# Attention and feed-forward on one core: prologue dealt out anew, late q moved, six weight chunks loaded as fp32 and cast on VectorE and GpSimd

## The chip, the cores and the metric

The kernel runs on one core of a Trainium2 chip. The metric is the time of one execution on the device in microseconds (us). A core has TensorE (PE; its weight loads are shown apart as PEld), VectorE (DVE), ScalarE (ACT), GpSimd (POOL), SyncE (SP, which here only issues transfers) and 16 DMA engines. Two queues carry the data in the traces: the hardware queue, filled by SyncE, and the software queue, filled by GpSimd (31.87 and 4.98 MB in the kernel before). Each profile is of one execution; its span is some 1.7 us shorter than the device time of the same execution. Kernels are compared only within the same rounds.

## The reference, cut to what matters

```python
# q, k, v: (B=4, H=8, S=768, D=64) fp32; w_in: (512, 2048); w_out: (2048, 512)
k_sum = k.reshape(B, H, nb, 32, D).max(axis=3)      # nb = 24 blocks
v_sum = v.reshape(B, H, nb, 32, D).mean(axis=3)
# each query sees the keys at a distance under 16, and all 24 block summaries (+ log 32)
a = softmax([where(mask_l, scores_l, -1e9), scores_s + log(32)])
attn_out = a @ concat(v, v_sum)
x = attn_out.transpose(0, 2, 1, 3).reshape(3072, 512)
h = x @ w_in
g = h * (1 / (1 + exp(-1.702 * h)))
out = g @ w_out                                     # (3072, 512) fp32
```

## The kernel before

The work is cut into eight units, each half a sequence of one batch. The attention of the first half has no other work to hide behind; this "prologue" ends near 23 us. Then each unit runs the first product ("ph", 64 matmuls of 128x384) and the second ("po", 48 matmuls of 128x512 in 12 slots of four), and the attention of the next half sits between these slots. In unit 0 the slots go by parts: all three row blocks use the first w_out chunk, then all three the second, and so on, because the chunks arrive one after another.

Weights come through the software queue. The load itself changes fp32 to bf16 on its way (such a load writes 512.0 KB a chunk in the kernel before):

```python
def load_w_in(c):                    # 4 chunks of 512 columns
    pool.dma_start(out=w_in_sb[:, :, c*512:(c+1)*512], in_=wi[:, :, c*512:(c+1)*512])
def load_w_out(c):                   # 4 chunks of 512 rows
    pool.dma_start(out=w_out_sb[:, c*4:(c+1)*4, :], in_=wo[:, c*4:(c+1)*4, :])
# ... after the hand-dealt prologue:
load_w_in(2)
for p in range(NP): load_q(0, p, 1)  # "late q": second half of batch 0's queries, fp32
load_w_in(3)
for c in range(4): load_w_out(c)
```

The late q is cast by VectorE, turned by TensorE against an identity, and copied out of PSUM by VectorE, all within unit 0's first product (after its columns 11 to 14). GpSimd issues every load of weights between its other instructions, in program order; in the traces here GpSimd and VectorE also work through their instructions in program order. `idle(n)` puts n small matmuls without use into TensorE's waits in the prologue; `busy(n)` does it with a PSUM tile of its own.

The loads of batch 1 stand behind a small copy whose only purpose is to wait for a late w_out chunk, so that they don't compete with the weights:

```python
if u == 0 and i == 1:
    sp.dma_start(out=hold, in_=w_out_sb[0:16, NT - 5, 0:16])   # third w_out chunk
    for p in range(NP): load_k(1, p)
    load_v(1)
```

The softmax here doesn't subtract the row's maximum and nothing guards it: scores larger than these inputs give would overflow.

## Time and profile before

| of the kernel before | value |
|---|---|
| median of runs (lowest to highest) | 221.47 us (221.15 to 221.71), 3 runs |
| profiled span, granted TensorE clock | 219.3 us, 1.000 |
| TensorE busy | 206.6 us, 94% |
| first "ph" matmul; first "po" matmul | 23.29 us; 37.19 us |
| hold copy; unit 1's first "ph" | 42.15 us; 50.67 us |
| waits of TensorE over 0.3 us in unit 0 | 0.40 + 0.79 + 0.35 us |

The table is read from the top down: TensorE is nearly always busy, so time can be won or lost only where it waits or where its instructions take longer. After 80 us neither happens. What a change to the start does to the end can therefore be read off at one instant, unit 1's first matmul at 50.67 us. The lines themselves stand in the prediction below.

### The profile page before, as it was taken

Reading aid. Unit: us, or ns where it says so; the run is one execution under the profiler, and the core shown is the slowest. Engines: PE = TensorE matmul, PEld = TensorE weight load, DVE = VectorE, ACT = ScalarE, POOL = GpSimd, SP = SyncE. Lnnn points to the kernel's source line nnn. Section 1 sums busy time; section 2 is a strip of 40 time slices with the busy share of each in tenths; the row PEclk is TensorE's granted clock in tenths of the full one; section 3 lists DMA queues with packets and bytes.
Section 4 is the critical chain, followed back from the end, with each engine's and each line's share of the span. In section 5 each row is a group of like instructions: output and inputs, shape, how many; then the busy total and the mean of one; then the engine's idle time right before and its main releaser. Section 6 shows DMA issues by size and latency. Waiting matters only on the chain.

```text
span 219.3 us, 4951 instructions
## 1 busy us (share of the span) xinstructions
PE 206.6 (94%) x1944; PEld 115.7 (53%) x1966; DVE 93.9 (43%) x261; ACT 136.9 (62%) x243; POOL 69.1 (32%) x169
## 2 busy tenths in 40 slices
PE   7679998999999999999999999999999999999994
PEld 3247554556655556454655465545554554555542
DVE  5997645345994830176707100549226001700000
ACT  3786775456577647862888277835786478637420
POOL 5579985014784029400600079004100000000000
PEclk9999999999999999999999999999999999999999
DMA  6999999999998999799699999998904300340012
GB/s 165 313 216 145 191 262 223 184 199 220 233 323 210 225 231 256 136 231 210 128 209 226 218 224 217 211 192 199 193 3 104 115 0 0 87 122 13 0 48 96
DMA packets 92710, 37.15 MB, mean 169 GB/s; under 512 B 77856, under 2 KB 89568, under 8 KB 92688
## 3 DMA queue, kind: packets, MB, share of 16 engines
q1 hardware_dynamic: 88272, 31.87, 71.2%
q0 software_dynamic: 4416, 4.98, 12.9%
q8 instruction: 15, 0.25, 0.5%
q14 instruction: 7, 0.06, 0.1%
HBM read 27.26 MB, written 6.29 MB: 153 GB/s over the span
## 4 chain that ended last, share of the span: by engine, by line
PE 81%; DMA 9%; SPq 3%; POOL 3%; issue 2%; DVE 1%; DVEq 0%; POOLq 0%
PE po L27 37%; PE ph L27 33%; DMA w_out_sb<-in_moe_w_out_dram 7%; PE ps_av L27 4%; SPq L27 3%; PE ps_s L27 3%; DMA vf<-in_v_dram 2%; PE ps_q L27 1%; POOL kx L27 1%; POOL vw L27 1%; PE ps_t L27 1%; DVE qT L27 1%; POOL w_in_sb L27 1%; PE ps_vs L27 1%; PE ps_x L27 1%
## 5 line engine op out<-in xcount | busy, mean ns | idle before, releaser
L27 PE MATMUL po<-w_out_sb,gT 128*128 128x512 bf16 (+2 forms) x378 | 86.3, 370 | 2.6 <-issue 1.6
L27 PE MATMUL ph<-xT,w_in_sb 128*128 128x384 bf16 x512 | 86.5, 326 | 0.8 <-DMA w_in_sb<-in_moe_w_in_dram 0.8
L27 ACT ACTIVATE gT<-ph 128x384 bf16<-128x384 f32 x128 | 60.9, 491 | 26.1 <-PE ph L27 26.0
L27 PEld LDWEIGHTS <-w_in_sb 128*128 128x128 bf16 x512 | 49.4, 98 | 33.3 <-DMA w_in_sb<-in_moe_w_in_dram 1.0
L27 PEld LDWEIGHTS <-gT 128*128 128x128 bf16 x400 | 36.3, 98 | 38.9 <-DMA w_out_sb<-in_moe_w_out_dram 0.7
L27 DVE TENSOR_TENSOR a_sb<-a_sb,mk 128x768 bf16<-128x768 bf16 x32 | 17.6, 555 | 66.5 <-ACT a_sb L27 65.4
L27 ACT ACTIVATE osb<-po 128x512 f32<-128x512 f32 (+1 forms) x24 | 14.2, 592 | 37.0 <-PE po L27 36.8
L27 ACT ACTIVATE a_sb<-ps_s 128x768 bf16<-128x768 f32 x32 | 24.2, 805 | 7.2 <-PE ps_s L27 7.2
L27 POOL CAST vw<-vf 128x768 bf16<-128x768 f32 (+3 forms) x36 | 24.8, 742 | 3.5 <-DMA vf<-in_v_dram 3.1
L27 ACT ACT_TABLE_LOAD x16 | 20.5, 1283 | 1.1 <-PEq L1029 0.8
L27 POOL COPY gate<-gT 128x1 bf16<-128x1 bf16 x4 | 0.8, 190 | 60.5 <-ACT gT L27 60.5
L27 POOL CAST kb<-kf 128x768 bf16<-128x768 f32 (+1 forms) x15 | 11.1, 766 | 17.6 <-DMA kf<-in_k_dram 17.6
L27 DVE TENSOR_TENSOR x<-ps_av,rc 128x384 bf16<-128x384 f32 x28 | 15.6, 558 | 1.0
L27 PEld LDWEIGHTS <-a_sb 128*64 128x64 bf16 x384 | 7.9, 111 | 6.9 <-issue 4.0
L27 DVE TENSOR_REDUCE ks<-kx 128x24 bf16<-128x768 bf16 x12 | 11.3, 939 | 0.1
L27 DVE COPY osb<-po 128x128 f32<-128x128 f32 x1 | 0.3, 292 | 24.9 <-PE po L27 24.9
L27 DVE COPY kx<-kx 128x80 bf16<-128x80 bf16 (+4 forms) x48 | 10.6, 272 | 0.0
L27 PE MATMUL ps_av<-vw,a_sb 128*64 128x65 bf16 x384 | 9.9, 198 | 0.5 <-DVE x_sb L27 0.5
L27 PE MATMUL ps_s<-qT,kx 64*128 64x64 bf16 x384 | 9.3, 191 | 1.0 <-POOL kx L27 0.6
L27 PEld LDWEIGHTS <-kx 64*128 64x128 bf16 x384 | 7.0, 95 | 5.4 <-issue 3.9
L27 DVE RECIPROCAL rc<-ps_av 128x6 f32<-128x6 f32 x32 | 6.1, 190 | 8.1 <-PE ps_av L27 8.1
L27 POOL CAST qb<-qf 128x768 bf16<-128x768 f32 (+1 forms) x13 | 8.9, 716 | 0.9 <-PE ps_q L27 0.8
(71 smaller groups left out, 126.1 us busy)
## 6 DMA issues: line engine op xcount, KB each, us to landing
out_dram<-osb SPq DMA_DIRECT2D x23, 256.0 KB, 3.1
kf<-in_k_dram SPq DMA_DIRECT2D x12, 384.0 KB, 5.7
vf<-in_v_dram SPq DMA_DIRECT2D x12, 384.0 KB, 5.7
qf<-in_q_dram SPq DMA_DIRECT2D x8, 384.0 KB, 5.7
w_in_sb<-in_moe_w_in_dram POOLq DMA_DIRECT2D x4, 512.0 KB, 7.6
w_out_sb<-in_moe_w_out_dram POOLq DMA_DIRECT2D x4, 512.0 KB, 17.1
kf<-in_k_dram SPq DMA_DIRECT2D x8, 192.0 KB, 4.0
qf<-in_q_dram SPq DMA_DIRECT2D x8, 192.0 KB, 3.8
```

Of the source, the lines that this page charges most:

```text
L27: r = f(*a, **kw)
```

## The change

It has three parts, called P, Q and W here.

- **P**: the prologue's casts, copies and turns are dealt out anew between the engines, and the values and x get PSUM tiles of their own. GpSimd reaches its first weight load sooner.
- **Q**: the late q is loaded behind the first w_out chunk, and its four turns move from the first product into slots 1 and 2 of the second. Their copies out of PSUM go to VectorE (turns 0 and 2) and ScalarE (1 and 3).
- **W**: two w_in chunks and all four w_out chunks are loaded as they are, in fp32, into the memory that held k, q and v of batch 0, and cast there by VectorE (both w_in chunks, w_out 0 and 1) and GpSimd (w_out 2 and 3). The apparent intent is to take the conversion out of the software queue and the weights off its critical path.

```diff
+    raws = stage.tile([128, 3 * NP * PR], F32, name="raws")      # k, q, v of all loads
+    room = {("i", 2): 0, ("i", 3): 2048, ("o", 0): 4096, ("o", 1): 6144, ("o", 2): 0, ("o", 3): 4096}
+    def cast_w_in(eng, c):      # 4 casts of 4 x 128 columns
+    def cast_w_out(eng, c, n=2):
     def load_w_out(c):
-        pool.dma_start(out=w_out_sb[:, c * 4:(c + 1) * 4, :],
+        pool.dma_start(out=roomy("o", c),
  ... (prologue: P, some 130 lines re-ordered)
-    load_w_in(2)
+    load_w_in(2, True)
+    load_w_in(3, True)
+    load_w_out(0)
     for p in range(NP):
         load_q(0, p, 1)
-    load_w_in(3)
-    for c in range(4):
-        load_w_out(c)
  ... (v casts on GpSimd)
+    load_w_out(1)
     vrows0()                    # block rows of v, and the halo and sum copies within SBUF
+    cast_w_in(dve, 2)
+    load_w_out(2)
  ... (key halos, pairs 0 and 1)
+    cast_w_in(dve, 3)
  ... (key halos, pairs 2 and 3)
+    cast_w_out(dve, 0)
+    load_w_out(3)
+    for p in range(NP):
+        cast_q(dve, p, 1)
+    cast_w_out(dve, 1)
     finish_masks()              # GpSimd
  ... (clears on GpSimd)
+    cast_w_out(pool, 2)
+    cast_w_out(pool, 3, 1)
-    plan0 = {0: ["s0", "s1"], 4: ["v0", "s2"], 6: ["x0", "s3"], 9: ["v1"], 11: ["x1"]}
+    plan0 = {1: ["q0", "q1"], 2: ["q2", "q3"], 3: ["s0", "s1"], 5: ["v0", "s2"], 7: ["x0", "s3"],
+             9: ["v1"], 11: ["x1"]}
+            elif what[0] == "q":
+                q_turn(i, 1)
+                q_copy(i, act if i % 2 else dve, 1)
-                sp.dma_start(out=hold, in_=w_out_sb[0:16, NT - 5, 0:16])
+                sp.dma_start(out=hold, in_=w_out_sb[0:16, NT - 7, 0:16])
```

More of the change, by code (lines that the diff above doesn't have):

```diff
@@ L81 @@
     raw, late = {}, [None]
+    PR = 2 * NJ * D
+    raws = stage.tile([128, 3 * NP * PR], F32, name="raws")
     def chunks(x, b, p):
@@ L87, in load_k @@
     def load_k(b, p):
-        t = stage.tile([128, 2, 2, JH, D], F32, name=f"kf{p}", tag=f"kf{p}")
+        t = (raws[:, p * PR:(p + 1) * PR]
+             .rearrange("p (h e r d) -> p h e r d", h=2, e=2, r=JH))
         if b:
@@ L99, in load_q @@
         if half is None:
-            t = stage.tile([128, 2, NJ, D], F32, name=f"qf{p}", tag=f"qf{p}0")
+            t = (raws[:, (NP + p) * PR:(NP + p + 1) * PR]
+                 .rearrange("p (h j d) -> p h j d", h=2, j=NJ))
             sp.dma_start(out=t.rearrange("p h j d -> p (h j) d"), in_=chunks(q, b, p))
@@ L109, in load_q @@
         t = (late[0][:, p] if half else
-             stage.tile([128, 2, JH, D], F32, name=f"qf{p}0", tag=f"qf{p}0"))
+             raws[:, (NP + p) * PR:(NP + p) * PR + PR // 2]
+             .rearrange("p (h r d) -> p h r d", h=2, r=JH))
         raw["q", p, half] = t
@@ L119, in load_v @@
         for p in range(NP):
-            t = stage.tile([128, 2, NJ, D], F32, name=f"vf{p}", tag=f"vf{p}")
+            t = (raws[:, (2 * NP + p) * PR:(2 * NP + p + 1) * PR]
+                 .rearrange("p (h j d) -> p h j d", h=2, j=NJ))
             if b:
@@ L237, in clear0, with roomy, load_w_in @@
             eng.memset(v6[g * 32:g * 32 + nb, :, g, D:D + 1], float(block))
-    def load_w_in(c):
+    room = {("i", 2): 0, ("i", 3): 2048, ("o", 0): 4096, ("o", 1): 6144, ("o", 2): 0, ("o", 3): 4096}
+    def roomy(kind, c):
+        o = room[kind, c]
+        return raws[:, o:o + 2048].rearrange("p (a n) -> p a n", a=4)
+    def cast_w_in(eng, c):
+        for i in range(4):
+            o = c * 512 + i * 128
+            copy(eng, w_in_sb[:, :, o:o + 128], roomy("i", c)[:, :, i * 128:(i + 1) * 128])
+    def cast_w_out(eng, c, n=2):
+        for i in range(0, 4, n):
+            copy(eng, w_out_sb[:, c * 4 + i:c * 4 + i + n, :], roomy("o", c)[:, i:i + n])
+    def load_w_in(c, plain=False):
         wi = moe_w_in.rearrange("(ko ki) n -> ki ko n", ki=128)
-        pool.dma_start(out=w_in_sb[:, :, c * 512:(c + 1) * 512],
+        pool.dma_start(out=roomy("i", c) if plain else w_in_sb[:, :, c * 512:(c + 1) * 512],
                        in_=wi[:, :, c * 512:(c + 1) * 512])
@@ L323, in idle, with opened @@
     def idle(n):
-        if st.get("idle") is None:
+        bank = st.get("idle")
+        if bank is None:
+            bank = next((t for t in two if any(t is r for r in read)), None)
+        if bank is None:
             return
         for i in range(n):
-            pe.matmul(out=st["idle"][:, 0:128], lhsT=warm[:, 0:128], rhs=warm[:, 0:128],
+            pe.matmul(out=bank[:, 0:128], lhsT=warm[:, 0:128], rhs=warm[:, 0:128],
                       start=True, stop=True)
+    two, read = [], []
+    def opened(t):
+        two.append(t)
+        del two[:-2]
     def busy(n):
@@ L458, in s_turn @@
         big = st["S", p] = psb.tile([128, 1024], F32, name="ps_s", tag="big")
+        opened(big)
         score_tiles(big, p, 0, 0)
@@ L473, in s_exp @@
                        func=ACT.Exp, scale=scale)
+        read.append(st["S", p])
     def s_mask(p, eng):
@@ L490, in b_exp @@
         act.activation(out=ab, in_=st["B", g][:, 0:HALF], func=ACT.Exp, scale=scale)
-        if g:
-            st["idle"] = st["B", g]
     def v_own(p, hh, eng):
@@ L525, in pv_of @@
     def pv_of(p):
-        return (st["V", p // 2][:, p % 2 * 512:p % 2 * 512 + 390]
+        return (st["V", p][:, 0:390]
                 .rearrange("p (h j c) -> p h j c", h=2, j=JH))
     def av_near(p):
-        if p % 2 == 0:
-            st["V", p // 2] = psb.tile([128, 1024], F32, name="ps_av", tag="big")
+        if p == 0:
+            st["idle"] = None
+        st["V", p] = pmm.tile([128, 512], F32, name="ps_av", tag="mm")
         for hh in range(2):
@@ L557, in x_turn @@
         src = x_sb.pop(p)
-        if p == 0:
-            if st.get("idle") is st["Q", NP - 1]:
-                st["idle"] = None
-            st["X", 0] = pmm.tile([128, 2, HALF], BF16, name="ps_x", tag="mm")
-        elif p == 2:
-            st["X", 1] = (psb.tile([128, 2048], BF16, name="ps_x2", tag="big")[:, 0:2 * HALF]
-                          .rearrange("p (i c) -> p i c", i=2))
+        st["X", p] = psb.tile([128, 2048], BF16, name="ps_x", tag="big")
+        opened(st["X", p])
         for j in range(JH):
-            pe.transpose(out=st["X", p // 2][:, p % 2, j * 128:(j + 1) * 128],
+            pe.transpose(out=st["X", p][:, j * 128:(j + 1) * 128],
                          in_=src[:, j].rearrange("p h d -> p (h d)"), identity=ident)
@@ L682, in ff_in @@
             act.activation(out=gT[u % 2][:, nt, :], in_=ph, func=ACT.Gelu_apprx_sigmoid)
-    N0 = 3
+    N0 = 2
     ph0, seen = [], []
@@ L747 @@
     warmth(8)
-    cast_k(act, 0, 0)
-    cast_k(pool, 2, 0)
+    cast_k(dve, 0, 0)
     cast_k(dve, 0, 1)
     k_turn(0)
-    cast_k(pool, 2, 1)
-    k_own(0, act)
-    cast_k(dve, 1, 0)
-    cast_k(dve, 1, 1)
-    k_turn(1)
-    k_own(1, act)
-    cast_k(act, 3, 0)
-    k_turn(2)
-    k_own(2, act)
-    cast_q(act, 0, 0)
+    cast_k(pool, 1, 0)
+    cast_k("dve_alone", 1, 1)
+    k_turn(1)
+    k_own(0, act)
+    cast_k(dve, 2, 0)
+    cast_k(pool, 2, 1)
     k_sides(0, pool)
     cast_k(pool, 3, 1)
+    k_own(1, act)
@@ L765 @@
+    k_turn(2)
+    k_max(0)
+    k_blocks(0, dve)
+    cast_k(act, 3, 0)
+    k_sides(1, pool)
+    k_own(2, act)
+    k_max(1)
+    cast_q(pool, 1, 0)
+    cast_q(act, 0, 0)
+    k_sides(2, pool)
     k_turn(3)
-    k_max(0)
+    k_own(3, act)
+    k_blocks(1, dve)
     q_turn(0)
-    k_blocks(0, dve)
-    cast_q(act, 1, 0)
     q_turn(1)
-    k_max(1)
-    k_blocks(1, dve)
-    k_sides(1, pool)
-    k_own(3, act)
+    q_copy(0, act)
+    cast_q(pool, 3, 0)
     k_max(2)
+    cast_q(dve, 2, 0)
@@ L776 @@
+    k_blocks(2, pool)
+    q_turn(2)
+    k_max(3)
     q_copy(1, act)
-    cast_q(dve, 2, 0)
-    q_copy(0, dve)
-    q_turn(2)
-    k_sides(2, pool)
     s_turn(0)
-    k_max(3)
+    k_sides(3, dve)
+    q_turn(3)
     q_copy(2, act)
-    s_exp(0)
-    k_blocks(3, dve)
-    k_blocks(2, pool)
-    cast_q(pool, 3, 0)
-    v_even(0, "dve_alone")
-    b_turn(0)
-    s_turn(2)
-    v_own(0, 0, pool)
-    v_own(0, 1, pool)
-    q_turn(3)
-    s_mask(0, dve)
-    s_turn(1)
-    q_copy(3, dve)
-    s_exp(2)
@@ L798 @@
-    b_turn(1)
-    s_exp(1)
-    b_turn(2)
-    v_own(1, 0, pool)
-    s_mask(2, dve)
-    v_sum(0)
-    v_own(1, 1, act)
-    k_sides(3, pool)
-    s_mask(1, dve)
-    v_copy(0, act)
-    b_turn(3)
-    idle(3)
-    s_turn(3)
-    v_before(0, "dve_alone")
-    load_w_in(0)
-    v_own(2, 0, pool)
-    v_even(1, act)
-    b_exp(0)
-    v_after(0, "dve_alone")
-    v_before(1, "dve_alone")
-    v_own(2, 1, act)
-    idle(4)
-    v_sum(1)
-    v_copy(1, dve)
-    idle(6)
-    av_near(0)
-    v_own(3, 0, "dve_alone")
@@ L825 @@
-    v_after(1, pool)
-    av_blocks(0, 0, D + 1)
+    s_turn(1)
+    k_blocks(3, pool)
+    b_turn(0)
+    b_turn(2)
+    v_own(0, 1, pool)
+    s_exp(0)
+    v_own(0, 0, dve)
+    b_turn(1)
+    q_copy(3, dve)
+    s_mask(0, dve)
+    v_sum(0)
+    s_turn(2)
+    s_exp(1)
+    b_exp(0)
+    v_own(1, 0, act)
+    b_turn(3)
+    v_copy(0, act)
+    v_before(0, "dve_alone")
+    s_turn(3)
+    v_even(0, pool)
+    v_after(0, "dve_alone")
+    v_before(1, act)
+    v_own(1, 1, "dve_alone")
+    av_near(0)
@@ L827 @@
+    av_blocks(0, 0, D + 1)
+    load_w_in(0)
+    s_mask(1, dve)
+    v_even(1, "dve_alone")
+    s_exp(2)
+    load_w_in(1)
+    v_before(2, pool)
+    v_sum(1)
+    v_copy(1, act)
+    v_own(2, 1, "dve_alone")
+    v_after(1, "dve_alone")
+    s_mask(2, dve)
+    v_own(2, 0, act)
     v_even(2, act)
-    v_before(2, pool)
-    idle(4)
+    v_own(3, 0, pool)
+    b_exp(1)
+    idle(11)
     v_sum(2)
-    load_w_in(1)
-    v_norm(0)
     av_near(1)
-    b_exp(1)
-    idle(3)
+    v_after(2, pool)
@@ L836 @@
+    v_copy(2, dve)
     av_blocks(1, 0, D + 1)
     s_exp(3)
-    v_own(3, 1, dve)
-    idle(5)
+    v_own(3, 1, pool)
+    av_near(2)
+    v_sum(3)
+    av_blocks(2, 0, D + 1)
+    v_norm(0)
     x_turn(0)
-    v_copy(2, act)
+    s_mask(3, dve)
     v_even(3, act)
-    idle(4)
-    v_sum(3)
+    v_before(3, act)
+    v_after(3, pool)
+    v_copy(3, act)
     v_norm(1)
-    v_after(2, pool)
-    v_after(3, act)
-    idle(3)
-    av_near(2)
-    idle(2)
-    x_turn(1)
-    v_before(3, pool)
-    av_blocks(2, 0, D + 1)
@@ L854 @@
-    v_copy(3, act)
-    s_mask(3, dve)
-    av_near(3)
-    copy(dve, xT[0], st["X", 0 // 2][:, 0 % 2])
-    gelu_soon()
-    copy(act, xT[1], st["X", 1 // 2][:, 1 % 2])
-    av_blocks(3, 0, D + 1)
+    v_norm(2)
+    idle(1)
+    av_near(3)
+    av_blocks(3, 0, D + 1)
+    gelu_soon()
+    copy(act, xT[0], st["X", 0][:, 0:HALF])
+    x_turn(1)
     ff_first(0)
-    v_norm(2)
+    copy(act, xT[1], st["X", 1][:, 0:HALF])
+    v_norm(3)
     x_turn(2)
-    copy(act, xT[2], st["X", 2 // 2][:, 2 % 2])
@@ L865 @@
-    v_norm(3)
+    x_turn(3)
+    copy(dve, xT[2], st["X", 2][:, 0:HALF])
+    copy(dve, xT[3], st["X", 3][:, 0:HALF])
     ff_first(1)
-    x_turn(3)
-    copy(dve, xT[3], st["X", 3 // 2][:, 3 % 2])
     ff_first(2)
     ff_first(3)
-    load_w_in(2)
+    load_w_in(2, True)
+    load_w_in(3, True)
+    load_w_out(0)
     for p in range(NP):
         load_q(0, p, 1)
-    load_w_in(3)
-    for c in range(4):
-        load_w_out(c)
     for p in range(NP):
         pool.tensor_copy(out=rows_of(0, p)[:, JH:NJ, 0], in_=raw_v(p)[:, JH:NJ])
+    load_w_out(1)
@@ L879 @@
     vrows0()
-    for p in range(NP):
+    cast_w_in(dve, 2)
+    load_w_out(2)
+    for p in range(2):
         key_halos(p, 0, dve, JH)
         key_rows(p, 0, ks0[p], dve, JH)
+    cast_w_in(dve, 3)
+    for p in range(2, NP):
+        key_halos(p, 0, dve, JH)
+        key_rows(p, 0, ks0[p], dve, JH)
+    cast_w_out(dve, 0)
[3 more added lines that the diff above has]
+    cast_w_out(dve, 1)
     finish_masks()
@@ L941 @@
         todo = {}
-        if u == 0:
-            for p in range(NP):
-                cast_q(dve, p, 1)
-                todo[11 + p] = [lambda p=p: (q_turn(p, 1), q_copy(p, dve, 1))]
-        elif u == 1:
+        if u == 1:
             s = 1
```

## The prediction

> **What bounds the kernel now.** I read the page's table of engines first, then the chain of waits, then the timelines of single engines up to 72 us, then the traffic of the DMA queues in half-microsecond stretches.
>
> ```profile
> span 219.3 us, 4951 instructions
> PE 206.6 (94%) x1944; PEld 115.7 (53%) x1966; DVE 93.9 (43%) x261; ACT 136.9 (62%) x243; POOL 69.1 (32%) x169
> ...
> PE po L27 37%; PE ph L27 33%; DMA w_out_sb<-in_moe_w_out_dram 7%; PE ps_av L27 4%; SPq L27 3%; PE ps_s L27 3%; DMA vf<-in_v_dram 2%; PE ps_q L27 1%; POOL kx L27 1%; POOL vw L27 1%; PE ps_t L27 1%; DVE qT L27 1%; POOL w_in_sb L27 1%; PE ps_vs L27 1%; PE ps_x L27 1%
> ```
>
> TensorE is busy 94% of the span, and 70% of the chain is the two feed-forward products. From 78.84 us to 216.2 us the chain is TensorE alone but for short issue gaps, unit after unit of the same work; the change touches nothing there. Only the first 70 us can move: the attention of the first half sequence (to 23.3 us), the first feed-forward unit (to 50.7 us), and the entry of batch 1. In the chain in order of time that part reads:
>
> ```profile
> 8.79 5.42 DMA vf<-in_v_dram
> ...
> 21.93 0.73 POOL w_in_sb L27
> 22.66 14.49 DMA w_out_sb<-in_moe_w_out_dram
> 37.19 0.39 PE po L27
> ```
>
> The second product ("po") starts at 37.19 us because the first w_out chunk lands then. TensorE's own timeline shows how little it really lost to that, 0.79 us on the fourth w_in chunk and 0.35 us on w_out, since the first product filled the time:
>
> ```profile
> 33.56 0.82 PE L27 MATMUL ph<-xT,w_in_sb 128*128 128x384 bf16 x4 [0.79 <-DMA w_in_sb<-in_moe_w_in_dram]
> ...
> 37.19 1.04 PE L27 MATMUL po<-w_out_sb,gT 128*128 128x512 bf16 x3 [0.35 <-DMA w_out_sb<-in_moe_w_out_dram]
> ```
>
> In half-microsecond stretches the software DMA queue (all weights and the late q) moves 101 packets at its best, each 2 KB of fp32 read and 1 KB of bf16 written: about 410 GB/s read. In the stretch that is nearly all late q (27.5 to 28.5 us), which is not cast, it writes about 375 GB/s. From 17.0 to 19.0 us hardly anything flows: v has ended and the first w_in chunk, issued at 16.34, has only begun. After that the DMA engines are full to 43 us.
>
> Batch 1 is the other constraint. Its k loads wait for w_out's third chunk (the little "hold" copy at 42.15), and GpSimd then follows the loads:
>
> ```profile
> 42.15 0.61 SPq L27 DMA_DIRECT2D hold<-w_out_sb  x1
> 42.80 5.25 SPq L27 DMA_DIRECT2D kf<-in_k_dram  x4
> ```
> ```profile
> 47.36 0.82 POOL L27 CAST kb<-kf 128x768 bf16<-128x768 f32 x1 [11.21 <-DMA kf<-in_k_dram]
> ...
> 57.28 5.07 POOL L27 CAST vw<-vf 128x768 bf16<-128x768 f32 x6 [1.09 <-DMA vf<-in_v_dram]
> 62.29 0.50 POOL L27 CAST qb<-qf 128x384 bf16<-128x384 f32 x1
> ```
>
> The sums over v's blocks run on TensorE at 62.07 us; the last cast they need ends near 61.5. So this chain has about 0.6 us of slack: what delays the loads of batch 1 by more than that delays TensorE.
>
> [...] the trace has 1.29 us for four casts, 0.32 each, [...] the same GpSimd copy pair takes 0.64 us at 7.90 and 1.58 us at 14.80, where VectorE multiplies two SBUF tensors (masks) from 14.88 to 15.89.
>
> **The change part by part.**
>
> *Prologue.* The pieces of k, q and v work are dealt out anew between engines; the products are the same, 22 fewer idle matmuls among them. GpSimd loses one pair of key-side copies (about 0.6 to 1.6 us) and a v cast before its first w_in issue, and gains a q cast. Adding its queue up with measured durations (casts 0.51, copy pairs 0.64, waits for k(3) at 9.2 and v at 13.4 as before) gives a first issue near 14.4 us in place of 16.34, and the second right behind it instead of at 18.58. This fills the hole from 17 to 19 us: about 1.7 us earlier for every weight after it. The late q goes behind the first w_out chunk: 0.79 MB, 2 us at 0.39 MB/us, earlier for the fourth w_in and the first w_out chunk, nothing for the second w_out chunk and later. Landing in the changed kernel, from about 33.5, 37.15 and 39.6 now (the last from issue plus landing time): fourth w_in about 29.8, first w_out 32.5 to 33.5, second w_out 37.5 to 38.
>
> *VectorE casts.* [...] They stand in one line with the key halos, 0.74 + 0.19 + 0.93 + 0.18 = 2.04 us for the first two pairs and 1.3 for the other two. Third w_in landed at about 26.8: cast to 28.35, halos to 30.4, fourth w_in to 31.95, halos to 33.25, first w_out to 34.6, late q (4 x 0.32) to 35.9, second w_out 37.7 to 39.0.
>
> *TensorE in unit 0.* If the first product starts at 22 to 23 us (it may: v's end at 18.5 us allows it), its 64 matmuls at 163 ns are 10.4 us and four transposes and waits some 1.2: done by 34 to 34.6. The casts of w_in are ready one piece ahead of it. "po" starts at 34 to 34.6, some 2.6 us earlier than now. Part of it is only moved: the late q turns (4 x 0.33 = 1.3 us) left the first product and now stand between matmuls of the second, in its slots 1 and 2.
>
> *The new wait.* The third q turn needs a PSUM buffer that the copy of the first frees. That copy is VectorE's, and in VectorE's order it comes after the casts of the second w_out chunk: 39.0 + 0.80 = 39.8. TensorE is there at 34.3 + 3 x 0.866 + 0.66 = 37.6, so it waits some 2.2 us, of which about 0.9 it would have waited for that chunk anyway. From 39.8 the rest of the unit is 0.66 (q) + 9 x 0.866 + 2.65 (scores, values, transposes, as now) = 11.1, so 50.9, plus 0.4 for GpSimd's casts: 51.3 against 50.67 now. The gained 2.6 us are gone.
>
> *GpSimd.* It issues the fourth w_out load after the first chunk's cast (34.6 + 0.75 = 35.4), then the masks (28.91 to 34.43 now: 5.5 us) and the clears (1.7): 42.6. A cast of 768 takes 0.83, of 384 0.51, so 1024 about 1.05 and 512 about 0.6: third chunk 43.6 and 44.7, fourth 45.3 to 47.1. The third is wanted at about 44, the fourth at 47.5.
>
> *Batch 1.* The hold copy waits for the first of these casts, 43.6 against 42.15: 1.5 us later. Some comes back, because the weights no longer hold the DMA engines then (the last weight packets of now flow until 43): the first k about 48.1 in place of 47.36, 0.75 us later. Less the slack of 0.6 that is 0.15; TensorE's own 0.6 later is the larger of the two and decides. In sum **about +0.6 us: 222.0 us**.
>
> **The rivals.**
> 1. *The prologue's gain survives.* If the second w_out chunk lands 2 us sooner than I think, the q turn waits for nothing and unit 0 ends near 49. For it: 17 to 19 us is a true hole. Against it: batch 1 still waits for GpSimd's casts, which hang on VectorE's line plus 9 us of masks, so at most about 1.5 us is kept: 220.
> 2. *Plain loads are slow.* At 375 GB/s instead of 410 the six chunks (6.3 MB) take 1.4 us more, and the second w_out chunk comes near 39; the waits on GpSimd and VectorE add: 224. For it: the late q's rate. [...]
> 3. [...] the third w_out cast ends near 46, and the loads of batch 1 slip by 2.5 us more: 224 to 225. For it: the stretched copies. Against it: VectorE has under 4 us of casts during the masks.
> 4. *The shared tile ties loads together* beyond the true overlaps. In the changed program only overlapping regions wait, so I give it nothing.
>
> **Range and chances.** All of these lie within 4.4 us (2%) of now: rival 1 is -1.5, rivals 2 and 3 +2.5 to +3.5. Two of them together could pass +4.4; for -4.4 the whole prologue gain and more would have to survive two chains that I see bound. So 219.6 to 224.8 for 8 in 10; faster by over 2% 0.04, within 0.90, slower 0.06.
>
> **What would show it.** Right: first w_in issue near 14.4; no hole in the software queue at 17 to 19; first po matmul near 34.5; TensorE waiting 1.5 to 2.5 us on a DVE copy of q before the third late q turn; unit 1's first ph at 51 to 51.5; hold near 43.6. Wrong: [...] if po starts after 36, if hold comes before 42, or if the first product starts after 24.5. From 80 us on, one unit must take 23.1 to 23.6 us as now; if it doesn't, something I left out has changed.

The forecast's sum came to 222.0 us, 0.6 above the kernel before. The times of VectorE's weight casts in the text allow 1.55 us for a w_in chunk and 1.3 us for a w_out chunk, and 1.73 and 1.43, 1.30 and 1.39 us were measured afterwards. That plain loads can gain nothing in rate was not shown; the sum took the rate as unchanged, as the author's assumption, and an argument about row sizes against rival 2 is gone with it. How VectorE might hold up GpSimd was not shown either, beyond the copy pair that took 1.58 us for 0.64; it gave rival 3 and was no term of the sum.

## The result, and the profile after

The changed kernel took 227.72 us (median of 4 runs, 227.06 to 229.01) against 221.33 us (4 runs, 221.15 to 221.71). The ratio is 1.029, with a 95% interval of 1.024 to 1.035: slower by 2.9%. Here and below a ratio is the mean time of one kernel's fast runs over the mean of the other's fast runs of the same rounds, so it is not quite the ratio of the medians quoted. Executions over 1.5% slower than the fastest of the same kernel are left out of the means. The prediction said 222.0 us, within 2%, and a range up to 224.8. The measured time lies outside both.

The head of the page and its chain of waits, of the kernel after:

```profile
span 226.5 us, 4959 instructions
PE 210.3 (93%) x1944; PEld 116.1 (51%) x1944; DVE 96.5 (43%) x272; ACT 137.9 (61%) x244; POOL 74.9 (33%) x175
...
PEclk9999999759999999999999999999999999999999
```

The row of the granted clock (40 slices of 5.66 us, in tenths) has a dent at 40 to 51 us. Before, all 40 digits were 9. The busy times of TensorE, 206.6 and 210.3 us, should not be compared: both pages count 1944 matmuls, but only because the trace of the kernel before lacks 22 records of "po" (378 of 400), while the kernel after really has 22 fewer idle matmuls (its weight loads are 1944 against 1966).

TensorE's timeline of the kernel after (start, duration, engine, operation, tiles, count, and in brackets the idle time before it and what ended that):

```profile
36.29 2.05 PE L27 MATMUL po<-w_out_sb,gT 128*128 128x512 bf16 x8 [1.40 <-DVE w_out_sb L27]
39.25 0.65 PE L27 MATMUL ps_q<-ident,qb 128*128 128x128 bf16 x6 [0.91 <-DVE qb L27]
...
43.93 0.48 PE L27 MATMUL ps_q<-ident,qb 128*128 128x128 bf16 x3 [2.79 <-DVE qT L27]
44.20 1.91 PE L27 MATMUL po<-w_out_sb,gT 128*128 128x512 bf16 x4
...
57.75 1.46 PE L27 MATMUL ph<-xT,w_in_sb 128*128 128x384 bf16 x8
```

Three waits, 5.10 us in sum, stand in unit 0, where the kernel before had 0.40, 0.79 and 0.35 us, 1.5 in sum. (Two more gaps there, 0.16 us each and marked "issue", come before 7 recorded "po" where the kernel has 8: a record is missing.) Each of the three is for VectorE: a cast of a weight chunk, a cast of the late q, a copy of a turned q. Note also the four "po" matmuls at 44.20: 1.91 us, where 8 of them at 36.29 took 2.05.

The chain of waits in order of time (start, duration, what) says what VectorE was waiting for:

```profile
24.89 1.74 POOL vw L27 x4
26.68 15.08 DMA raws<-in_moe_w_out_dram
41.78 1.39 DVE w_out_sb L27 x2
43.17 0.71 DVE qT L27
43.93 0.48 PE ps_q L27 x3
44.40 1.71 PE po L27 x4
46.11 0.75 PE ps_s L27 x24
46.86 3.32 PE po L27 x8
```

The second w_out chunk is issued at 26.68 us and lands at 41.78. Before, the same chunk landed near 39.6 us (estimated from its issue and the median landing time) and needed no cast. Behind its two casts in VectorE's queue stands the copy of the first turned q, and TensorE's fourth turn waits for the PSUM buffer that this copy frees. The third turn, at 40.81 us, apparently got the buffer of the second, which ScalarE had copied by 40.75.

The last two lines carry the other half. Later in the same chain, at 50.97 us, 8 "po" matmuls take 1.83 us; here they take 3.32. The windows view (stretch, length, busy time and count of PE, PEld, DVE, ACT and POOL, then granted clock, DMA share, GB/s):

```profile
39.60:43.00 3.40, 1.50 (x10) 0.74 (x11) 1.75 (x4) 0.81 (x1) 2.91 (x10) 1.00 1.03 389
44.00:45.00 1.00, 1.00 (x5) 0.49 (x5) 0.52 (x1) 0.56 (x1) 0.89 (x13) 0.50 0.74 279
50.00:51.00 1.00, 1.00 (x38) 0.79 (x38) 0.24 (x2) 0.00 (x0) 0.96 (x2) 1.00 1.27 288
```

In the 3.4 us before 43.0 TensorE was busy 1.50 us. Then its clock was halved. From narrower windows (0.62 in 43.0 to 43.1, 0.57 in 49 to 50) the half clock lasted from 43.02 to 49.86 us, 6.84 us.

**Where the 7.1 us come from.** Unit 1's first matmul is at 57.75 us against 50.67. The first product starts at 23.88 us instead of 23.29: 0.6 us. Waits in unit 0 are 5.1 us instead of 1.5: 3.6 us. The half clock makes the turns, "po" and scores between 43.9 and 50.2 us some 2.7 us longer (4 "po" 1.71 for 0.87, 8 "po" 3.32 for 1.83, and about 0.4 in the small ones). The sum is 6.9 us; the last 0.2 is not placed. The spans differ by 7.2: from there on the two traces run in parallel.

The loads of batch 1 are late too, in SyncE's own timeline:

```profile
47.13 0.61 SPq L27 DMA_DIRECT2D hold<-w_out_sb  x1
47.85 4.61 SPq L27 DMA_DIRECT2D raws<-in_k_dram  x4
```

But they decide nothing. GpSimd's last v cast of batch 1 ends at 66.9 us, and TensorE begins the sums over v at 69.18 (before: 62.07), 2.3 us later, at the place in its queue.

Why did the weights land late? In GpSimd's timeline of the kernel after:

```profile
20.13 0.63 POOL L27 CAST vw<-raws 128x384 bf16<-128x384 f32 x1 [1.03 <-DMA raws<-in_v_dram]
...
21.76 1.51 POOL L27 DMA_DIRECT2D raws<-in_moe_w_in_dram  x2
```

The first two w_in chunks are issued at 14.62 us and just after, so the hole at 17 to 19 us is gone. But GpSimd then waits for the last pieces of v, and issues the third and fourth at 21.76 us. A new hole opens at 22 to 24 us, in which the engines move 111 and 105 GB/s.

Afterwards the plain loads are slower than the casting ones for a while. The traffic of the two queues between 31 and 37 us (packets, MB written, share of the 16 engines), first before:

```profile
q0 software_dynamic: 1013, 1.00, 99.9%
q1 hardware_dynamic: 408, 0.34, 21.9%
```

and after:

```profile
q0 software_dynamic: 406, 1.60, 86.2%
q1 hardware_dynamic: 317, 0.26, 17.1%
```

A casting load reads two bytes for each one that it writes, so the 1.00 MB before are 2.00 MB of fp32 weights read. The plain loads, of weights and late q, got through 1.60 MB in the same time, 20% less. The hardware queue carries the halo and sum copies of v within SBUF there.

### The profile page after: what moved, and what is told of

Read it like the earlier page. It is cut to its first block, busy times and chain, and to the rows that moved or that the text cites. A ratio compares the mean times of both kernels' runs of the same rounds, so it can differ in the third digit from the quotient of the medians.

```text
span 226.5 us, 4959 instructions
## 1 busy us (share of the span) xinstructions
PE 210.3 (93%) x1944; PEld 116.1 (51%) x1944; DVE 96.5 (43%) x272; ACT 137.9 (61%) x244; POOL 74.9 (33%) x175
## 4 chain that ended last, share of the span: by engine, by line
PE 78%; DMA 9%; SPq 6%; POOL 2%; DVE 2%; issue 1%; DVEq 0%; POOLq 0%
PE po L27 37%; PE ph L27 32%; DMA raws<-in_moe_w_out_dram 7%; SPq L27 6%; PE ps_av L27 3%; PE ps_s L27 3%; DMA raws<-in_v_dram 3%; POOL vw L27 1%; DVE qT L27 1%; PE ps_q L27 1%; PE ps_t L27 1%; POOL raws L27 1%; DVE w_out_sb L27 1%; PE ps_vs L27 1%; PE ps_x L27 1%
## 5 line engine op out<-in xcount | busy, mean ns | idle before, releaser
L27 PE MATMUL po<-w_out_sb,gT 128*128 128x512 bf16 (+2 forms) x400 | 92.1, 378 | 1.4 <-DVE w_out_sb L27 1.4
L27 PE MATMUL ph<-xT,w_in_sb 128*128 128x384 bf16 x512 | 85.6, 326 | 1.3 <-ACT xT L27 1.3
L27 DVE TENSOR_TENSOR a_sb<-a_sb,mk 128x768 bf16<-128x768 bf16 x32 | 19.1, 601 | 66.3 <-ACT a_sb L27 65.1
L27 POOL CAST vw<-raws 128x768 bf16<-128x768 f32 (+4 forms) x35 | 25.0, 769 | 4.3 <-DMA raws<-in_v_dram 3.5
L27 POOL CAST kb<-raws 128x768 bf16<-128x768 f32 (+1 forms) x15 | 11.1, 766 | 8.1 <-DMA raws<-in_k_dram 8.1
L27 POOL CAST qb<-raws 128x768 bf16<-128x768 f32 (+1 forms) x14 | 9.4, 697 | 3.2 <-issue 2.9
L27 ACT ACTIVATE qT<-ps_q 128x384 bf16<-128x384 f32 (+1 forms) x7 | 6.0, 858 | 7.3 <-PE ps_q L27 7.2
L27 DVE COPY kx<-kx 128x80 bf16<-128x80 bf16 (+4 forms) x50 | 9.4, 240 | 0.0
```

The costliest lines, as they stand in the source:

```text
L27: r = f(*a, **kw)
```

## The experiments

My first theory after the trace was: W makes the second w_out chunk late, the q copy stuck behind its cast makes TensorE wait, and the wait costs a second time by halving the clock. The rivals: P or Q is the cause; the two plain w_in chunks are; contention between VectorE and GpSimd is; or the loss needs Q's place for the q turns. Runs 1 to 8 were made on one chip, 9 to 12 on another, 13 and 14 on a third. All were correct. Edits are against the kernel after unless another is named.

One caution for all that follows: a single profile does not fix a landing time to better than about 1 us. The kernel after and kernels 1, 2 and 6 issue the same loads in the same order, yet VectorE's cast of the second w_out chunk starts at 41.78, 42.97, 40.70 and 40.62 us in their profiles.

### 1. Keep TensorE warm in the q wait

```diff
             elif what[0] == "q":
+                if i == 2:
+                    busy(44)
                 q_turn(i, 1)
```

> 44 idle matmuls (about 2.5 us) stand where TensorE waits 2.79 us for the third late q turn. If the granted clock of 0.50 from about 43 to 49.4 us follows from that idle time, the clock stays at 1.0 there and the kernel gains about 2.7 us: 225.0. If the throttle has another cause [...], the clock dips all the same and the time stays at 227.7 or grows a little.

Measured: 227.30 us (226.03 to 228.09), ratio 1.023 (1.015 to 1.030), span 226.4. A miss. The half clock is gone from 43 us, but has appeared in the prologue, at a wait that was 1.31 us in the profile of the kernel after and is longer in this one. TensorE's timeline:

```profile
22.09 0.80 PE L27 MATMUL ps_vt<-vw,E 128*64 128x128 bf16 x6 [2.32 <-POOL vw L27]
```

Six of these sums take 0.80 us instead of 0.50: they run at half clock (0.50 from 22.1 to 22.5 us). The run did not isolate what it was made for.

### 2. All late q copies on ScalarE

```diff
-                q_copy(i, act if i % 2 else dve, 1)
+                q_copy(i, act, 1)
```

> All four late q copies on ScalarE, so that no copy stands behind VectorE's casts of the second w_out chunk. Theory of the copy's place: the third q turn starts near 40.8 instead of 43.93, TensorE then waits only for the chunk's first cast at about 42.5, idles about 1 us at a time, keeps its clock: 223 to 224. Rival, the landing of the second w_out chunk (41.78) is the whole wait: the time stays above 226.5.

Measured: 227.36 us (225.80 to 228.58), ratio 1.025 (1.017 to 1.032). In the profile the q wait is gone (the last turns are at 39.51 and 40.04 us), TensorE waits 1.08 us for the chunk itself, no half clock follows, and the span is 224.1, 2.4 us less. But the chunk's cast also starts 1.08 us earlier (40.70), which the edit does not touch. The mean of the runs does not show a gain, and 223 to 224 was expected. The trace confirms the path; the time is inconclusive.

### 3. W undone, P and Q kept: all weights cast by the DMA

```diff
     def load_w_in(c, plain=False):
+        plain = False
     def load_w_out(c):
-        pool.dma_start(out=roomy("o", c),
+        pool.dma_start(out=w_out_sb[:, c * 4:(c + 1) * 4, :],
-    cast_w_in(dve, 2) ... cast_w_out(pool, 3, 1)     (all six cast calls)
```

> The six chunks are cast by the DMA as before, straight into the weights; new order of the prologue, late q moved and issue order stay. If the fp32 loads are the loss (slower beside the halo copies, casts, their waits, the late hold copy), the first w_out lands by 34, po starts near 35, the hold copy comes by 41 and the time is 219 to 221.5. If the order of issue and the late q are the loss, it stays above 225.

Measured: 222.46 us (220.69 to 223.08), ratio 1.0015 (0.995 to 1.008), span 219.0. TensorE's timeline:

```profile
33.29 1.90 PE L27 MATMUL po<-w_out_sb,gT 128*128 128x512 bf16 x7
36.95 0.61 PE L27 MATMUL ps_q<-ident,qb 128*128 128x128 bf16 x6 [1.76 <-DVE qb L27]
```

The second product starts at 33.29 us, 3.0 us earlier than after, without a wait. One wait is left, 1.76 us for the late q. So W carries the loss, and P with Q are worth nothing that these runs resolve (the interval is -0.5 to +0.8%): what P gains in front, the wait for the moved q largely takes. The time missed the 219 to 221.5 us expected.

### 4. Third and fourth w_in load issued before GpSimd's wait for v

```diff
     v_even(2, act)
+    load_w_in(2, True)
+    load_w_in(3, True)
     v_own(3, 0, pool)
  ... (and not at their old place)
```

> The two plain w_in loads are issued before GpSimd's three last v casts, near 17.5 instead of 21.76 us. If the hole in the software queue at 22 to 24 us is a cause, every later weight lands about 1.5 us earlier (second w_out near 40.3) and the time falls by about 1.5 us to 226, or by more if the idle time gets short enough to keep the clock (223). Rival: v's tail lands later by as much, the first product starts later, and the time stays within 0.5 us of 227.7.

Measured: 226.09 us (224.48 to 227.75), ratio 1.019 (1.012 to 1.027), span 224.9. The third w_in load is issued at 17.32 us instead of 21.76, and the second w_out chunk's cast starts at 39.98 us, 1.8 us earlier than after and below all four profiles with the old order (40.62 to 42.97). So the hole at 22 to 24 us did cost landing time; the size is good to about 1 us only (the w_in casts start just 0.5 us earlier). TensorE still waits 3.04 us for the q copy, and a half clock of some 3.4 us falls on the start of the first product (0.6 in that slice of the page's clock row, 0.992 over the span), so little of it reaches the end.

### 5. Halo and sum copies after the second w_out chunk

```diff
     def vrows0():
  ...
+    def halos0():
         w5 = vw[0].rearrange("p (j e) h c -> p j e h c", e=2)
  ...
     cast_w_out(dve, 1)
+    hold2 = consts.tile([16, 16], BF16, name="hold2")
+    sp.dma_start(out=hold2, in_=w_out_sb[0:16, 4, 0:16])
+    halos0()
```

> The six small copies inside the SBUF (halo rows and block sums of v) wait until the second w_out chunk has landed; the rest is the changed kernel. If fp32 loads lose their rate beside these copies (0.73 to 0.88 MB in 3 us there against 1.16 alone), the second w_out chunk lands near 39.5 to 40 in place of 41.78, the third late q turn starts 2 us earlier and TensorE keeps its clock: 223 to 225. If the rate is the DMA's own there, the landing stays within 0.5 us of 41.8 and the time within 1 us of 227.

Measured: 226.08 us (224.77 to 227.00), ratio 1.021 (1.014 to 1.027), span 223.1. The queue between 31 and 37 us, with no copies beside it:

```profile
q0 software_dynamic: 570, 2.22, 102.9%
```

The plain loads now move 2.22 MB instead of 1.60 in these 6 us, 0.37 MB/us, and VectorE's cast of the second chunk starts at 39.61 us instead of 41.78. The rate repeats: in these 6 us the seven profiles with plain w_out loads beside copies (after, kernels 1, 2, 4, 6, 8, 10) show 1.54 to 1.67 MB, the two without copies (5 and 11) 2.22 and 2.21. So it is the copies beside them that slow them: the two queues take 86.2 and 17.1% of the same 16 engines' time in the kernel after. VectorE's casts, which might have held up GpSimd's queue, are not: VectorE is busy 3.91 us of this stretch here, where the loads are fast, and 2.69 in the kernel after. The 2.2 us of landing are less sure, since the loads were also issued 0.8 us earlier here. That 0.26 MB of copies takes the room of 0.62 MB of loads is measured. The casting loads gave way too, but less: at their rate alone (0.62 MB written in 3 us, before, 37 to 40 us) they would have read some 2.5 MB in 6 us, by estimate, and they read 2.00 beside 0.34 MB of copies. Why the plain ones lose more is not settled. The time was expected lower: the q wait is still 2.48 us, and a half clock of some 3.4 us follows it (0.992 over the span).

### 6. Warm in three places

```diff
     av_near(2)
+    idle(24)
     v_sum(3)
  ...
+                if i == 2:
+                    busy(44)
                 q_turn(i, 1)
  ...
         if u == 0:
+            busy(20)             # before the second product
```

> Idle matmuls in all three long waits: 24 before the last v sum, 20 before the second product, 44 before the third late q turn. In the first of these experiments with idle matmuls the half clock only moved to another gap (2.32 us before the last v sum). If idle time sets the clock, no run of this kernel shows a stretch at half clock, the runs lie closer together, and the mean falls to 224 to 225. If not, half clock appears in runs of it as often as before and the time stays 226 to 228.

Measured: 226.50 us (225.38 to 229.71), ratio 1.019 (1.012 to 1.026), span 223.6. The clock is 0.997 to 1.000 in all four runs, against 0.976 to 0.992 of the kernel after. In the profile unit 1 starts at 54.76 us, 3.0 us earlier. Of this 1.1 us is already there at the fourth turn (42.82 for 43.93 us: the chunk landed earlier); the other 1.9 come after it, where the half clock is gone and a wait of 0.70 us for a masked score tile has come. The three fast runs, 225.4 to 226.8 us, lie above the 224 to 225 expected. One run took 229.71 us at clock 0.997 and is slow; it isn't explained.

### 7 and 8. Only w_in plain; only w_out plain

Kernel 7:

```diff
     def load_w_out(c):
-        pool.dma_start(out=roomy("o", c),
+        pool.dma_start(out=w_out_sb[:, c * 4:(c + 1) * 4, :],
  ...
-    cast_w_out(dve, 0)
-    cast_w_out(dve, 1)
-    cast_w_out(pool, 2)
-    cast_w_out(pool, 3, 1)
```

Kernel 8:

```diff
     def load_w_in(c, plain=False):
+        plain = False
  ...
-    cast_w_in(dve, 2)
-    cast_w_in(dve, 3)
```

> Only the two w_in chunks stay fp32 loads with VectorE casts; the four w_out chunks are cast by the DMA. If the loss comes from w_out (loads beside the halo copies, the late cast ahead of the q copy, GpSimd's casts and the hold copy behind them), this is 221.5 to 223. If each chunk costs alike, a third of the loss remains: 224.

Measured for 7: 222.86 us (222.07 to 223.83), ratio 1.005 (0.999 to 1.011), span 221.6.

> Only the four w_out chunks stay fp32 loads; w_in is cast by the DMA. If w_out is the loss: 226 to 228, like the changed kernel. If each chunk costs alike, two thirds remain: 225.

Measured for 8: 227.69 us (226.11 to 228.35), ratio 1.024 (1.017 to 1.032), span 226.7, clock 0.984 or 0.985 in all four runs. TensorE's timeline has the same wait as the kernel after:

```profile
44.17 0.48 PE L27 MATMUL ps_q<-ident,qb 128*128 128x128 bf16 x3 [2.80 <-DVE qT L27]
```

With P and Q in place, the w_out loads alone bring the loss; the w_in loads alone cost about half a per cent, with an interval that includes nothing at all.

### 9. W undone, w_in loads issued early

Against kernel 3:

```diff
     v_even(2, act)
+    load_w_in(2)
+    load_w_in(3)
     v_own(3, 0, pool)
  ...
-    load_w_in(2, True)
-    load_w_in(3, True)
     load_w_out(0)
```

> Six chunks cast by the DMA, and the last two w_in loads issued before GpSimd's last three v casts. If the hole in the software queue counts, all later weights and the late q land about 1.3 us earlier than with DMA casts alone (late q cast near 35.2 in place of 36.53), the wait of 1.76 us before the first late q turn shrinks to about 0.5, and the kernel beats the one before by 0.5%: about 220. Rival: v's tail lands later, the first product starts later by as much: no change against the casts by DMA alone (ratio 1.00).

Measured: 220.67 us (220.01 to 221.68), ratio 0.997 (0.994 to 1.000), span 218.3. TensorE's timeline, and the windows around:

```profile
19.75 0.35 PE L27 MATMUL ps_av<-vw,a_sb 128*64 128x65 bf16 x11 [1.26 <-POOL vw L27]
```

```profile
16.60:20.00 3.40, 1.87 (x41) 1.44 (x39) 3.24 (x8) 2.67 (x6) 3.11 (x6) 1.00 1.23 201
22.00:24.00 2.00, 1.54 (x20) 1.14 (x17) 1.02 (x3) 1.87 (x4) 2.00 (x5) 0.50 1.24 206
```

Here the clock was halved from 20.06 to 26.88 us although no gap was longer than 1.26 us. What is low is the share: TensorE was busy 1.87 of the 3.4 us before. Four of the six runs show a clock of 0.983 or 0.984, two kept 0.998 or 0.999.

### 10. W alone, in the kernel before

The edit, against the kernel before, is W with the old prologue and the old places of the q turns. No q copy stands behind a w_out cast.

```diff
-    load_w_in(2)
+    load_w_in(2, True)
     for p in range(NP):
         load_q(0, p, 1)
-    load_w_in(3)
-    for c in range(4):
-        load_w_out(c)
+    load_w_in(3, True)
+    load_w_out(0)
  ... (load_w_out(1), cast_w_in(dve, 2), load_w_out(2), halos, q casts, halos)
+    cast_w_in(dve, 3)
     finish_masks()
  ... (after the first product's last column:)
+        cast_w_out(dve, 0)
+        load_w_out(3)
+        cast_w_out(dve, 1)
+        cast_w_out(pool, 2)
+        cast_w_out(pool, 3, 1)
```

> The kernel before with only the fp32 loads and casts added: its prologue, its late q in the first product (q copies ahead of the w_out casts on VectorE). If the loads alone bring the loss whatever the order, 224 to 227. If the loss needs the late q moved behind the casts (the copy of q waiting behind the second w_out chunk), this stays within 1% of before: 221 to 223.5.

Measured: 225.85 us (225.59 to 225.92), ratio 1.020 (1.017 to 1.023), span 224.1. TensorE's timeline:

```profile
35.93 1.31 PE L27 MATMUL ph<-xT,w_in_sb 128*128 128x384 bf16 x4 [3.52 <-DVE w_in_sb L27]
```

The loss is there without P and Q, but at another wait: the fourth w_in chunk landed at 35.40 us instead of 33.5 and its cast comes on top; then the clock is halved for some 3.4 us (0.50 from 36.3 us, 0.992 over the span). So the chunk that TensorE waits for here is one of w_in. The rival "it needs Q's place for the turns" falls. The q copy behind the cast is the form that the loss takes in the changed kernel, not its root.

### 11. The changed kernel with three mends

The edits of 2, 4 and 5 together:

```diff
+    load_w_in(2, True)            # before v_own(3, 0, pool)
+    load_w_in(3, True)
+    sp.dma_start(out=hold2, in_=w_out_sb[0:16, 4, 0:16])     # after cast_w_out(dve, 1)
+    halos0()
-                q_copy(i, act if i % 2 else dve, 1)
+                q_copy(i, act, 1)
```

> fp32 loads kept, with the three mends together: w_in issued early, halo copies after the second w_out chunk, late q copies on ScalarE. If hole, halo copies and the copy behind the cast are the causes, the wait before the third late q turn goes, no stretch at half clock is left, and the time is 221 to 223. If something else in the loads costs (GpSimd's casts, the late hold copy), it stays above 224.

Measured: 223.47 us (223.15 to 224.22), ratio 1.010 (1.007 to 1.013), span 222.5. The second w_out cast starts at 37.36 us, the q wait is down to 0.32, and a new one comes, for the copies that were put off:

```profile
44.39 0.19 PE L27 MATMUL ps_av<-vw,a_sb 128*64 128x65 bf16 x1 [2.76 <-DMA vw<-vs]
```

Two thirds of the loss are mended with W in place. Half clock (some 3.4 us; 0.992 over the span) follows this wait as well, and both that and the time miss what was expected.

### 12. Kernel 9 with the q turns one slot later

```diff
-    plan0 = {1: ["q0", "q1"], 2: ["q2", "q3"], 3: ["s0", "s1"], 5: ["v0", "s2"], 7: ["x0", "s3"],
-             9: ["v1"], 11: ["x1"]}
+    plan0 = {2: ["q0", "q1"], 3: ["q2", "q3"], 4: ["s0", "s1"], 6: ["v0", "s2"], 8: ["x0", "s3"],
+             10: ["v1"], 11: ["x1"]}
```

> As the early issue with DMA casts, and the late q turns, scores and values of the next half one slot later (0.87 us), so that the late q is there in time. If the wait for the late q is what is left, TensorE waits less than 0.3 us there and this is 0.2 to 0.5 us faster than without the shift; if the later values then hold up the last transposes, it is as much slower.

Measured: 221.73 us (221.02 to 224.27), ratio 1.003 (0.999 to 1.007). A miss: there is no q wait, but no gain either. The last transposes now come close to the end of the unit and wait 0.35 us for VectorE, and the clock was 0.976 to 0.984 in all six runs.

### 13. Kernel 9 with matmuls in its two waits

```diff
     v_own(3, 1, pool)
+    idle(22)
     av_near(2)
+    idle(6)
     v_sum(3)
```

> DMA casts with the early issue, and 22 + 6 idle matmuls in the waits before the third pair's values and the last v sum, where that kernel's profile went to half clock from 20.1 to about 27 us. If the clock follows the idle time, the half clock in the prologue goes, the first product ends about 2 us sooner, the wait for the late q takes back about 1 us of it, and the time is 219 to 220 (ratio 0.990 to 0.994), faster than both. If the clock has another cause, it dips again and the ratio stays at 0.997.

Measured: 220.29 us (219.33 to 220.70), ratio 0.996 (0.992 to 0.999), span 217.6. In the page:

```profile
PEclk9999999999999999999999999999999999999999
```

TensorE is busy 3.13 of the 3.40 us from 16.6 to 20.0, where kernel 9 had 1.87, and the clock stays at 0.998 to 1.000 in all six runs. This version beats both kernels: P and Q with casting loads, issued early, and warm. It is 0.4% faster than the kernel before and, by the two ratios to it, some 3.3% faster than the changed one. The clock did what was expected; the time, at 0.990 to 0.994, did not, and against kernel 9's 0.997 (0.994 to 1.000) the gain from the clock is not resolved.

### 14. The kernel before without its idle matmuls

```diff
     def idle(n):
-        if st.get("idle") is None:
-            return
+        return
```

> The kernel before with all its 40-odd idle matmuls of the prologue taken out, nothing else changed; no data hangs on them. If idle time of TensorE halves the clock, stretches at half clock appear between 15 and 30 us and the time grows by 0.5 to 2 us. If the throttle is not tied to idle time, the clock stays at 1.00 and the time stays as it is.

Measured: 221.57 us (220.66 to 221.78), ratio 1.000 (0.995 to 1.005), span 220.1. The clock is 0.982 to 0.984 in all four runs. The windows of this kernel:

```profile
14.80:18.20 3.40, 1.77 (x34) 1.07 (x33) 3.12 (x8) 2.88 (x9) 3.40 (x6) 1.00 0.87 174
20.00:22.00 2.00, 2.00 (x35) 1.74 (x29) 1.20 (x3) 0.75 (x2) 1.94 (x4) 0.50 1.24 207
```

Removing matmuls that do nothing is the only edit, and it brings the half clock. So idle time of TensorE brought the half clock here: in the same rounds the eleven runs of the kernel before show 0.992 to 1.000. Kernels 9 and 13 show the same from the other side. An increase of 0.5 to 2 us was expected, and none came, apparently because the first product waits for the fourth w_in chunk in any case (1.51 us at 34.82 us; that chunk also came later in this profile than in the one before, at 33.56).

## Why the prediction was wrong

**Right.** The first w_in issue came at 14.62 us (14.4 expected), and the old hole closed. The casts took 1.73 and 1.43 us for the w_in chunks and 1.30 and 1.39 for w_out (1.55 and 1.3 expected). The named wait exists, on VectorE's q copy behind the second w_out chunk's cast, though before the fourth turn, not the third. From unit 1 on nothing changed. Batch 1's loads did not decide the time: the hold copy was later than thought (47.13 for 43.6), with 2.3 us of slack left at the sums over v.

**The step that failed first: "Landing in the changed kernel".** It put the second w_out chunk at 37.5 to 38 us; it landed at 41.78. It carried the gain at GpSimd's first issue through to every weight after it, and took the rate of the loads as unchanged.
- GpSimd's queue has a second place where it stands in front of a load: the wait for v at 19 to 20 us, ahead of the third w_in issue. Kernel 4 took it away: 1.8 us.
- The rate was measured where plain loads run alone. In the stretch that decides, they run beside the copies within SBUF. Kernel 5 moved the copies: 2.2 us. Rival 2 had this direction, at 1.4 us for all six chunks and for a different reason.

These two together make up the misestimate of about 4 us: with both mended the cast starts at 37.36 us (kernel 11), where the prediction had it. How the 4 us divide between them is known to about 1 us only. Rival 3, VectorE and GpSimd in each other's way, decided nothing: GpSimd's five mask copies, beside VectorE's casts, took 2.15 us for 1.22, but no wait of TensorE in unit 0 is for GpSimd.

**The step "The new wait".** The mechanism was right; its size was not. TensorE waited 2.79 us there, not 2.2, and had already waited 1.40 us for the first w_out chunk's cast and 0.91 us for the late q, for which the prediction had nothing. The first product began at 23.88 us, not at 22 to 23, and "po" started at 36.29 us, beyond the 36 that the prediction itself had named as a sign of error.

**What was left out altogether: the clock.** The sum took each instruction's duration as fixed. Idle time had a price beyond itself: about 2.7 us in this trace. The granted clock fell to half (0.50) and stayed there for 6.84, 6.82 and 6.83 us in the profiles of the kernel after, kernel 9 and kernel 14; in those of kernels 4, 5, 10 and 11 it was about half as long (3.3 to 3.8 us, by the mean clock of 0.992 over their spans). It fell in or after gaps of 2.79 us (after), 2.32 (kernel 1) and 1.26 (kernel 9), and in kernel 14 with no gap over 0.82 us in the 3.4 us before. TensorE's busy share in the 3.4 us before, a stretch of about half the 6.8, was 1.50, 1.87 and 1.77 us (44, 55 and 52%) in the kernel after, kernel 9 and kernel 14; at 2.24 us (66%, kernel before, 14.0 to 17.4) nothing happened. A low share did not always do it: the kernel after had 1.53 us (45%) from 17.4 to 20.8 and kept its clock (1.00 to 27.6). What rule decides was not shown. The kernel before carries idle matmuls in its prologue, apparently for this reason; the prediction counted them and did not ask what they were for. That idle time causes the half clock here is shown by kernels 9 against 13 and before against 14. What it costs is read from durations in the traces; in means of runs it is not resolved (kernel 6: ratio 1.019, up to 1.026; kernel after: from 1.024; kernels 9 and 13, and before and 14, do not differ clearly either).

**Which part of the change it is.** W: kernels 3 (1.0015 without W) and 10 (1.020 with W in the kernel before). In the changed order it is the w_out loads (kernel 8: 1.024 with them alone); in the old order the longest wait, 3.52 us, is for a w_in chunk (kernel 10). A casting load already read 410 GB/s; a plain one reads the same bytes, no faster (390), and adds a cast in an engine's queue before the data can be used. By these rates there was nothing to gain in the transfer, and a late chunk to lose.

**Open.** The runs of the kernel after and of kernels 1, 2, 6 and 8 spread over 225 to 230 us, also where runs show no half clock (kernel 2: 227.93 us at clock 1.000); what the slower ones among them wait for was not seen. Kernels 10 and 11, on another chip, spread over only 0.3 and 1.1 us. Why plain loads lose more than casting ones beside the copies within SBUF stays open too.

## What to carry to other kernels

The conversion inside the load was free here (0.41 MB/us read with it: 0.62 MB written in 3 us, before, 37 to 40 us; 0.39 without: 1.16 MB in 3 us, after, 40 to 43 us); taking it out added a cast, and the cast stood in an in-order queue together with copies that others wait for. When an issue moves forward, follow the issuing engine's queue on to every later load, and ask what shares the DMA engines in the stretch that decides. Count TensorE's idle time twice: where waits left it 44 to 55% busy over 3.4 us, the next 6.8 us ran at half clock here in three profiles, and once, at 45%, they did not. Small matmuls in the wait kept the clock (kernel 13, 0.998 to 1.000 in all six runs); what that saves was not resolved in means of runs.
